# An S4D and SwiGLU block in which the rows' first inputs move into buffers whose contents are dead

## The chip, the cores and the metric

The kernel runs on one core of one Trainium2 chip, in one launch. The metric is the device time of that launch in microseconds (us). Before the change three runs gave a median of 976.74 us (975.26 to 977.07). Engines are TensorE (PE, with PEld for its weight loads), VectorE (DVE), ScalarE (ACT), GpSimd (POOL) and SyncE (SP), which here only issues DMAs. Each works through its own queue in order; between engines they wait on semaphores.

## The reference

One adaLN block over 2048 tokens of 640 channels, with 128 complex states for each channel and 1728 hidden units, all in fp32:

```python
mod = (silu(c) @ w_mod).reshape(1, 6, 1, -1)
sa, ca, ga, sb, cb, gb = mod rows
h = layernorm(x) * (1 + ca) + sa
K[d, l] = 2 Re sum_n C[d, n] dt[d] exp(A[d, n] dt[d] l)
y = irfft(rfft(h, 2L) * rfft(K, 2L))[:L] + h * D_skip
x = x + ga * y
h = layernorm(x) * (1 + cb) + sb
x = x + gb * ((silu(h @ w1) * (h @ w3)) @ w2)
```

The convolution runs along the tokens, the normalisations and the gated product along the channels. All of the first half (all channels' convolutions) for a token is needed before its second normalisation.

## The kernel before, in words

*Convolution.* The 640 channels are done in five blocks of 128 (b4 is the last, number 4). For each block the kernel's taps are made in eight chunks on POOL, ACT and DVE from exponential tables E (lines 517 and 565; one pair of tables for blocks of even number, one for odd), TensorE sums them over the states (kps), and the taps and the normalised input xb go through a first transform (ps), a spectrum (fh, fk), a product on DVE (hz, fp) and the first half of the inverse (fz). Its result zt is stored to HBM as zd, eight tiles for a block. xb, the spectral buffer sp, and the modulation rows rw lie in a pool named core.

*Rows.* The second half of the inverse works by tokens. zd is loaded again, token-wise. In the first part four inputs, iz0 to iz3 (u = 0 to 3, two row tiles each, so iy0 to iy7), serve token blocks 0 and 1 of 512 tokens each; TensorE multiplies them by wd (iy), DVE adds the result to the tokens x2 (ia), and statistics for the second normalisation are taken (BN, the is tasks). iy covers the channels of the first four channel blocks (cut = 512); the fifth block's 128 channels come last, by the reload izb0 and izb1, two loads of four DMAs each that wait for the last stores of zd, then iyb and iab. Then come the reciprocal root (rs), xn, the transposes tp, the modulation v, and the split of x into a high and a low part (x0h and x0l and so on), since each fp32 product is made of three: high by high, low by high, high by low.

*The feed-forward part.* Up tiles of 128 hidden units (numbers 0 to 12, and 13 with 64) are loaded raw (wr), split into wh and wl, and multiplied (gu); then th, a and ah are the gate, and acc the down product with w2, split likewise. The first two tiles (0 and 13) run plain for blocks 0 and 1 before all weights go through combined sums in larger groups.

*What sets the order.* Up to the start of those groups a list scheduler, Plan (line 167), decides: each task has an engine, a duration, predecessors, a rank (smaller goes first among those that are ready at nearly the same time) and rings of buffers that it takes and gives. Tasks of tail_tasks (line 1044) carry their ranks in the code. A tile framework then puts in the waits that data, buffers and reused memory require, so memory that is opened where another pool was closed waits for that pool's last reader. DMA issues use eight semaphores: a DMA on SP can wait for the landing of the eighth before it. Loads made by load (line 1060) are paced besides (line 1035): load n waits for the landing of load n-2 while n is under 6, then of load n-4, up to LOADS. Three steps structure the end of the plan: `change` closes the pools of the table work and opens xp, wp and ip for the rows; `border` closes ip, inv and core and opens the pools of the feed-forward part; in between run the last spectra.

Before the change, x2[0] and wd0 are loaded while block 4's chunks are made, everything else of the rows after `change`: iz0, iz1, up tile 0, up tile 13, x2[1], wd1, iz2 in this order, all paced (iz0 and iz1 are eight DMAs, an up tile two). iz3 goes after `border` into x3h and x3l, tiles of x that are not yet in use, so that iy6 and iy7 (u = 3) run after the transposes of block 0:

```python
early = j < 6
([] if early else ["tp0.4"]), rank if early else 16.7
```

x2 of block 1 is prepared by prepare(1, 31), that is with a rank behind the gates of block 0.

Of the kernel before, what the change touches and what calls it, by code (L numbers as in the profile page):

```python
# [10 lines left out]
F32 = mybir.dt.float32  # L11
F32R = mybir.dt.float32r
I32 = mybir.dt.int32
# [17 lines left out]
LOADS = 21  # L31
# [249 lines left out]
class K:  # L281
# [65 lines left out]
    def ln_end(self, pool, st, mv, tag):  # L347
# [169 lines left out]
    def table_sets(self):  # L517

        G = self.nc.gpsimd
        self.tabs, self.E = [], []  # L520
        self.j8 = self.tbl.tile([P, 8], F32, name="j8")
        for j in range(8):
            G.memset(self.j8[:, j:j + 1], float(j))
        for i in range(2):
            p1, p2 = (self.tbl.tile([P, HB2, 2, n], I32, name=f"p{n}{i}") for n in (8, 4))
            G.memset(p1[:, :, :, 0], 0)
            self.tabs.append((p1, p2))
            self.E.append((self.tbl.tile([P, P, 2, 8], F32, name=f"e1{i}"), self.tbl.tile([P, P, 3, 4], F32, name=f"e2{i}")))
        self.step = self.tbl.tile([P, 3, 2, HB2], I32, name="step")
# [514 lines left out]
    def tail_tasks(self, border, cut):  # L1044
# [15 lines left out]
        def load(name, src, dst, size, after=(), **kw):  # L1060
            i = n_load[0]
            n_load[0] += 1
            loads.append(name)
            early = i < LOADS
            add(name, "SP", 0, lambda: self.paced(dst(), src), ["change", *after] + (loads[max(i - 2, 0):i][:1] if early else ["izb0"]), -60 + .1 * i,
                dma=[size * (.62 if early else 1.0)], **kw)
        loads = []

        def load_x2(b):
            for q in range(4):  # L1070
                s = slice(q * 32, q * 32 + 32)
                load(f"lx{b}.{q}", self.xv[q, :, 4 * b:4 * b + 4, :], lambda b=b, s=s: self.x2[b][s], 327680)

        def load_wd(i):
            load(f"lwd{i}", self.t_wd[:, 4 * i:4 * i + 4], lambda: self.wd[i], 262144)
# [38 lines left out]
        for q in range(4):  # L1114
            s = slice(q * 32, q * 32 + 32)
            add(f"lx0.{q}", "SP", 0, lambda q=q, s=s: self.nc.sync.dma_start(self.x2[0][s], self.xv[q, :, :4, :]), [f"g{b4}.{q}.ph"], -400, dma=[327680])
        add("lwd0", "SP", 0, lambda: self.nc.sync.dma_start(self.wd[0], self.t_wd[:, :4]), [f"g{b4}.4.ph"], -400, dma=[262144])
        load_z(0)
        load_z(1)
        load_up(0)  # L1120
        load_up(13)
        load_x2(1)
        load_wd(1)
        load_z(2)

        def raw_split(m, rank, after=None):
            names = [f"lu{m}.{i}" for i in range(2)]
# [26 lines left out]
        def rows(b, rank):  # L1154
            for j in range(4 * b, 4 * b + 4):
                u = j // 2
                early = j < 6

                def inv(j=j, u=u, early=early):
                    py = bank[j] = self.pbank(f"iy{j}") if early else self.acc_bank(f"iy{j}", j % 4)  # L1160
# [4 lines left out]
                def plus(j=j):  # L1165
# [3 lines left out]
                    ([f"{x}{b4}.{i}.e" for x in ("hh", "k") for i in range(8)] if b == 0 else []) + (["z4.3.z"] if j in (4, 5) else []) + ([] if early else ["tp0.4"]), rank if early else 16.7, take=[("bank", 1)] if early else [])  # L1169
                add(f"ia{j}", "DVE", .69, plus, [f"iy{j}"], rank, give=[("bank", f"iy{j}")] if early else [])  # L1170
# [5 lines left out]
        add("border", None, 0, border, ends + [f"ia{j}" for j in range(6)] + ["change"], 0)  # L1176
# [23 lines left out]

        def ln_rest(b):
            ln[b] = self.ln_end(self.fp, *self.stats[b], f"n{b}")
# [9 lines left out]
        def prepare(b, rank):  # L1212
# [3 lines left out]
            add(f"ln{b}", "DVE", 3.9, lambda: ln_rest(b), [f"isb{b}"] + [f"is{j}.{c}" for j in range(4 * b, 4 * b + 4) for c in range(2)], rank)  # L1216
            for j in range(4):
                add(f"xn{b}.{j}", ("ACT", "DVE"), (.91, .62), lambda e, j=j: xn.__setitem__((b, j), self.norm(b, j, *ln[b], e)), [f"ln{b}"], rank + .01 * j)
            for k in range(KT):
                r = rank + .1 + .1 * k  # L1220
# [14 lines left out]
                add(f"tp{b}.{k}", "PE", .88, tp, [f"xn{b}.{j}" for j in range(4)] + [f"tp{b}.{k - 1}"] * (k > 0) + ([f"ia{4 + j}" for j in range(4)] + ["iab1"] if b else []), r)  # L1235
# [4 lines left out]
        prepare(1, 31)  # L1240

        def plain(b, tiles, p, rank, after):
# [23 lines left out]
            for r, m in enumerate(tiles):  # L1266
                gates(b, m, banks, f"{b}.{m}", last, names, (rank if b else 30) + .5 + .1 * r)
# [245 lines left out]
    def run(self):  # L1513
# [3 lines left out]
        self.wk, self.wz = c.tile([P, 2, P], F32, name="wk"), c.tile([P, 2, P], F32, name="wz")  # L1517
        self.dsk = c.tile([P, NB, E4], F32, name="dsk")
# [14 lines left out]
        core = self.core = open_("core", "right")  # L1533
        self.wb = core.tile([P, 32, P], F32, name="wb")
# [4 lines left out]
        self.wd = [x0.tile([P, 4, 2, 64], F32, name="wd0")]  # L1539
        self.x2 = [x0.tile([P, 4, D], F32, name="x20")]  # L1540
# [602 lines left out]
```

## Time and profile before

| What | Before |
|---|---|
| median of the runs | 976.74 us |
| lowest and highest of three | 975.26, 977.07 us |
| the profiled execution | 979.65 us |
| its span | 977.9 us |
| its mean granted TensorE clock | 0.969 |
| bytes moved | 127.31 MB |

The profiled execution is one run of its own; every duration that is quoted comes from it. In the rows a busy time is followed by "x" and the number of instructions, a timeline gives start, length and the group that ran, and the square bracket behind it gives the idle time of the engine just before, with what ended it. An operation is written out<-in by the program's names. The TensorE clock is the share of full speed that was granted.

### The profile page before, as it was taken

Reading aid. Unit: us, or ns where it says so; the run is one execution under the profiler, and the core shown is the slowest. Engines: PE = TensorE matmul, PEld = TensorE weight load, DVE = VectorE, ACT = ScalarE, POOL = GpSimd, SP = SyncE. Lnnn points to the kernel's source line nnn. Section 1 sums busy time; section 2 is a strip of 40 time slices with the busy share of each in tenths; the row PEclk is TensorE's granted clock in tenths of the full one; section 3 lists DMA queues with packets and bytes.
Section 4 is the critical chain, followed back from the end, with each engine's and each line's share of the span. In section 5 each row is a group of like instructions: output and inputs, shape, how many; then the busy total and the mean of one; then the engine's idle time right before and its main releaser. Section 6 shows DMA issues by size and latency. Waiting matters only on the chain.

```text
span 977.9 us, 20556 instructions
## 1 busy us (share of the span) xinstructions
PE 864.3 (88%) x7985; PEld 683.7 (70%) x7985; DVE 699.2 (72%) x1393; ACT 547.5 (56%) x1024; POOL 342.6 (35%) x371
## 2 busy tenths in 40 slices
PE   1463787779899997889999999999999999999997
PEld 1132665767788883667777778878778888888776
DVE  7998899999999957886767767557456464645322
ACT  6877788979888841564444445346434443443312
POOL 1797789879899600002112111000012112120000
PEclk9986898999999997899999999999999999999999
DMA  9955453623235269847345421265442323220374
GB/s 216 276 170 195 107 130 92 174 67 89 51 86 126 69 167 250 202 121 238 112 122 161 122 93 62 89 188 189 135 112 77 99 69 102 80 83 28 108 217 133
DMA packets 110506, 127.31 MB, mean 130 GB/s; under 512 B 10568, under 2 KB 90696, under 8 KB 109128
## 3 DMA queue, kind: packets, MB, share of 16 engines
q1 hardware_dynamic: 109032, 125.21, 45.3%
q8 instruction: 63, 1.03, 0.5%
q10 hardware_dynamic: 1376, 0.79, 0.3%
q14 instruction: 35, 0.29, 0.1%
HBM read 95.82 MB, written 30.15 MB: 129 GB/s over the span
## 4 chain that ended last, share of the span: by engine, by line
PE 70%; DVE 15%; ACT 6%; DMA 4%; issue 3%; POOL 1%; SPq 1%; DVEq 0%; ACTq 0%
PE c L156 19%; PE acc L156 18%; PE X L156 12%; PE ps L156 4%; PE gu L156 3%; DVE yy L156 3%; PE kps L156 3%; PE fk L156 3%; PE fz L156 2%; PE fh L156 2%; DVE hn L156 2%; DVE fp L156 2%; DVE xx L156 2%; ACT tr L156 2%; PE iy L156 1%
## 5 line engine op out<-in xcount | busy, mean ns | idle before, releaser
L156 PE MATMUL acc<-ah,w 128*128 128x512 f32 x560 | 173.2, 395 | 2.7 <-DMA w<-w2d 1.9
L156 PEld LDWEIGHTS acc<-ah,w 128*128 128x128 f32 x560 | 103.7, 188 | 26.1 <-issue 2.3
L156 PE MATMUL acc<-al,w 128*128 128x512 f32 x260 | 101.9, 392 | 0.0
L156 POOL TENSOR_TENSOR yy<-e,e 128x512 f32<-128x512 f32 x80 | 86.3, 1095 | 18.8 <-PE kps L156 15.2
L636 DVE TENSOR_TENSOR wl<-s,wh 128x256 fp32r<-128x256 f32 x92 | 38.9, 423 | 68.2 <-ACT wh L635 67.8
L812 POOL TENSOR_TENSOR s<-wr 128x256 f32<-128x256 f32 x22 | 16.7, 760 | 188.5 <-DVE wl L636 91.3
L635 ACT ACTIVATE wh<-s 128x256 fp32r<-128x256 f32 x92 | 37.6, 410 | 79.2 <-PE X L156 58.5
L156 POOL TENSOR_TENSOR ph<-p,p 128x1024 int32<-128x1024 int32 x40 | 78.9, 1972 | 6.7 <-ACT tr L156 6.4
L156 PE MATMUL kps<-yy,xx 128*32 128x64 f32 x2560 | 51.4, 234 | 29.0 <-DVE xx L156 21.4
L156 DVE TENSOR_TENSOR yy<-yy,tr 128x512 f32<-128x512 f32 (+1 forms) x80 | 75.4, 945 | 0.9 <-ACT tr L156 0.6
L156 PEld LDWEIGHTS kps<-yy,xx 128*32 128x32 f32 x2560 | 45.0, 117 | 38.9 <-issue 22.8
L635 ACT ACTIVATE wh<-wr 128x256 fp32r<-128x256 f32 x92 | 38.3, 418 | 56.5 <-PE X L156 43.2
L813 POOL TENSOR_TENSOR s<-s,wr 128x256 f32<-128x256 f32 x22 | 16.6, 754 | 133.2 <-issue 133.2
L873 ACT ACTIVATE t<-g 128x512 f32<-128x512 f32 x44 | 27.8, 632 | 52.7 <-DVE g L837 52.7
L156 ACT ACTIVATE tr<-ph,hpi 128x512 f32<-128x512 f32 x80 | 54.7, 691 | 3.9 <-DVE xx L156 2.2
L156 PEld LDWEIGHTS acc<-al,w 128*128 128x128 f32 x260 | 48.8, 188 | 11.0 <-DVE al L636 0.3
L842 DVE SCALAR_TENSOR_TENSOR g<-t,g 128x512 f32<-128x512 f32 x48 | 33.7, 702 | 31.3 <-ACT t L873 29.3
L156 DVE TENSOR_TENSOR xx<-tr,xx 128x512 f32<-128x512 f32 x80 | 54.5, 682 | 1.0 <-ACT tr L156 1.0
L156 ACT ACTIVATE tr<-ph 128x512 f32<-128x512 int32 x80 | 47.3, 598 | 13.2 <-DVE yy L156 7.4
L156 PE MATMUL ps<-wk,xb 128*64 128x128 f32 x640 | 48.1, 305 | 6.0 <-ACT sp L156 3.3
L156 PE MATMUL ps<-wk,ks 128*64 128x128 f32 x640 | 41.9, 283 | 12.9 <-DVE ks L156 8.1
L156 PEld LDWEIGHTS ps<-wk,xb 128*64 128x64 f32 x640 | 44.6, 221 | 10.8 <-ACT sp L156 4.6
(435 smaller groups left out, 2347.0 us busy)
## 6 DMA issues: line engine op xcount, KB each, us to landing
w<-w2d SPq DMA_DIRECT2D x42, 640.0 KB, 4.0
wr<-in_w SPq DMA_DIRECT2D x52, 320.0 KB, 3.9
zd<-zt SPq DMA_DIRECT2D x40, 256.0 KB, 3.0
w2d<-w SPq DMA_DIRECT2D x14, 640.0 KB, 3.6
xs<-in_x SPq DMA_DIRECT2D x16, 320.0 KB, 11.5
hs<-hb SPq DMA_DIRECT2D x20, 256.0 KB, 2.5
xb<-hs SPq DMA_DIRECT2D x20, 256.0 KB, 4.5
x<-in_x SPq DMA_DIRECT2D x16, 320.0 KB, 10.1
```

The costliest lines, as they stand in the source:

```text
L156: self.prev = self.k.order(f(*a, **kw), self.prev)
L635: self.nc.scalar.activation(H, v, AF.Copy)
L636: eng.tensor_tensor(Lo, v, H.bitcast(F32), op=ALU.subtract)
L812: eng.tensor_tensor(s[0], u[:, 0:2], u[:, 2:4], op=ALU.add)
L813: eng.tensor_tensor(s[1], s[0], g[:, 0:2], op=ALU.subtract)
L842: V.scalar_tensor_tensor(g, th, 1.0, g, op0=ALU.add, op1=ALU.mult)
L873: tanh = lambda o, i: A.activation(o, i, AF.Tanh, scale=0.5)
```

## The change

Three regions that are dead by then take data of the rows, and some tasks are put in another place:

- The tables of odd blocks, last used for block 3, now lie in a tile named late (3584 values for each partition) in pool x0. Behind block 3's last chunk this tile takes x2[1] (the first 2560) and wd0 and wd1. x2[0] is loaded while block 3's chunks are made, x2[1], wd0 and wd1 while block 4's are. wd2 and wd3 are issued right behind them.
- Up tile 0 is loaded raw into rw once the input of block 4 has been normalised, ahead of all iz, and its split no longer shares the ring wr.
- iz3 goes into xb, after the spectra of block 4 have been issued, so that iy6 and iy7 run with the other iy, before the reload; `border` waits for all eight ia and for the five splits of tile 0.
- wk, wz and dsk move from the pool const to core. LOADS is 20 in place of 21.
- The root of the normalisation is cut into steps (one task for block 0, four for block 1); prepare(1) gets rank 16.85, its transposes tp1 go by that rank and the rest of it one later; the gates of block 0's tiles 0 and 13 get rank 17 (G0); the sums T1 wait for these gates.

By the instruction order of the two builds, the engines' order stays as it was up to the last transforms of block 4, apart from the added loads on SP. There the five splits of tile 0 (ACT, DVE) stand among the last ps. tp1.0 stands after the fourth of the five steps of block 0's product, and tp1.1 to tp1.4 right after it; the 15 acc of the first down tile come behind block 1's product; on ACT the two high parts of w2 stand before xn of block 0, and the wh of tile 13 before the fifth hz of block 4.

```diff
-LOADS = 21
+LOADS = 20
+G0 = 17
...
+    def ln_mean(self, st, mv):
         for j in range(4):
             self.nc.vector.bn_aggr(mv[:, j, :], st[:, j, :, :])
+
+    def ln_end(self, pool, st, mv, tag):
+        self.ln_mean(st, mv)
         return self.rsqrt(pool, mv[:, :, 1], 4, tag, (mv[:, :, 0], -1.0))
+
+    def ln_steps(self, pool, mv, tag):
+
+        V = self.nc.vector
+        v, w, t = (pool.tile([P, 4], F32, name=f"rs_{x}_{tag}", tag=f"rs_{x}") for x in "vwt")
+        y, nb = (pool.tile([P, 4], F32, name=f"rs_{x}_{tag}", tag=f"rs_{x}", bufs=2) for x in "yn")
+        wi = w.bitcast(I32)
+
+        def first():
+            V.tensor_scalar(v, mv[:, :, 1], 1.0, EPS, op0=ALU.mult, op1=ALU.add)
+            V.tensor_scalar(wi, v.bitcast(I32), 1, None, op0=ALU.logical_shift_right)
+            V.tensor_scalar(wi, wi, -1.0, float(0x5F3759DF), op0=ALU.mult, op1=ALU.add)
+
+        def newton(i):
+            V.tensor_mul(t, w, w)
+            V.scalar_tensor_tensor(t, t, -0.5, v, op0=ALU.mult, op1=ALU.mult)
+            V.scalar_tensor_tensor(y if i == 2 else w, t, 1.5, w, op0=ALU.add, op1=ALU.mult)
+            if i == 2:
+                V.scalar_tensor_tensor(nb, mv[:, :, 0], -1.0, y, op0=ALU.mult, op1=ALU.mult)
+        return (y, nb), [first] + [lambda i=i: newton(i) for i in range(3)]
...
+            if i:
+                e = self.spare
+                self.E.append((e[:, :2048].rearrange("p (d m j) -> p d m j", m=2, j=8), e[:, 2048:].rearrange("p (d m j) -> p d m j", m=3, j=4)))
+            else:
+                self.E.append((self.tbl.tile([P, P, 2, 8], F32, name="e10"), self.tbl.tile([P, P, 3, 4], F32, name="e20")))
...
-                z[u] = [t.bitcast(F32) for t in self.x_new(f"x{u}", f"iz{u}", 2)]
+                z[u] = [self.xb[:, 1024 * pr:1024 * pr + 1024].rearrange("p (a d) -> p a d", a=2) for pr in range(2)]
-                    load(f"iz{u}.{pr}{h}", zv[:, t0:t0 + 2, :cut], dst, 262144, done + (["border"] if u > 2 else []))
+                    load(f"iz{u}.{pr}{h}", zv[:, t0:t0 + 2, :cut], dst, 262144, done + ([f"hh{b4}.{i}.m" for i in range(8)] if u > 2 else []))
...
+                    if m == 0:
+                        raw[m] = self.rw.rearrange("p a (k f) -> p a k f", k=KT)
...
-                     [f"wl{0 if m == 1 else 13}.{i}" for i in range(5 if m == 1 else 3)] if m in (1, 2) else [])
+                     [f"wl13.{i}" for i in range(3)] if m == 2 else [f"h{b4}.{i}.a" for i in range(4)] if m == 0 else [], "inv" if m == 0 else "change")
...
+        used = [f"g{b4 - 1}.7.z{i}" for i in range(3)] + [f"mag{b4 - 1}", f"exp{b4 - 1}"]
+        for b, src in ((0, b4 - 1), (1, b4)):
+            old = used if b else []
+            for q in range(4):
+                s = slice(q * 32, q * 32 + 32)
+                add(f"lx{b}.{q}", "SP", 0, lambda b=b, q=q, s=s: self.nc.sync.dma_start(self.x2[b][s], self.xv[q, :, 4 * b:4 * b + 4, :]),
+                    [f"g{src}.{q}.ph"] + old, -400, dma=[327680])
+            if b == 0:
+                continue
+            for i in range(2):
+                add(f"lwd{i}", "SP", 0, lambda i=i: self.nc.sync.dma_start(self.wd[i], self.t_wd[:, 4 * i:4 * i + 4]), [f"g{src}.4.ph"] + old, -400, dma=[262144])
+        load_up(0)
         load_z(0)
         load_z(1)
-        load_up(0)
         load_up(13)
-        load_x2(1)
-        load_wd(1)
         load_z(2)
+        load_z(3)
...
-                early = j < 6
-
-                def inv(j=j, u=u, early=early):
-                    py = bank[j] = self.pbank(f"iy{j}") if early else self.acc_bank(f"iy{j}", j % 4)
+
+                def inv(j=j, u=u):
+                    py = bank[j] = self.pbank(f"iy{j}")
...
-        add("border", None, 0, border, ends + [f"ia{j}" for j in range(6)] + ["change"], 0)
+        add("border", None, 0, border, ends + [f"ia{j}" for j in range(8)] + ["change"] + [f"wl0.{i}" for i in range(5)], 0)
...
-        load_z(3)
         load_down(0)
...
+            add(f"lm{b}", "DVE", .8, mean, [f"isb{b}"] + [f"is{j}.{c}" for j in range(4 * b, 4 * b + 4) for c in range(2)], rank)
+            if b == 0:
+                add("ln0", "DVE", 3.1, lambda: [f() for f in steps[0]], ["lm0"], rank)
+            for i in range(4 if b else 0):
+                add(f"ln{b}" if i == 3 else f"ln{b}.{i}", "DVE", .8 if i == 3 else .6, lambda i=i: steps[0][i](), [f"ln{b}.{i - 1}" if i else f"lm{b}"], rank + .01)
...
-                r = rank + .1 + .1 * k
+                r = rank + .1 + .1 * k + b
...
-        prepare(1, 31)
+        prepare(1, 16.85)
...
-                gates(b, m, banks, f"{b}.{m}", last, names, (rank if b else 30) + .5 + .1 * r)
+                gates(b, m, banks, f"{b}.{m}", last, names, (rank if b or m == 1 else G0) + .5 + .1 * r)
...
-            sums("T1", i, (1, 0), (0, 0), 41 + i, ["ia4", "ia5"])
-            sums("T2", i, (1, 2), "T1", 43 + i, ["ia6", "ia7"])
+            sums("T1", i, (1, 0), (0, 0), 41 + i, ["gl0.0", "gl0.13"])
+            sums("T2", i, (1, 2), "T1", 43 + i, [])
...
+        self.wk, self.wz = core.tile([P, 2, P], F32, name="wk"), core.tile([P, 2, P], F32, name="wz")
+        self.dsk = core.tile([P, NB, E4], F32, name="dsk")
...
-        self.wd = [x0.tile([P, 4, 2, 64], F32, name="wd0")]
-        self.x2 = [x0.tile([P, 4, D], F32, name="x20")]
+        self.spare = x0.tile([P, 3584], F32, name="late")
+        self.wd = [self.spare[:, 2560 + 512 * i:3072 + 512 * i].rearrange("p (a b c) -> p a b c", a=4, b=2) for i in range(2)]
+        self.x2 = [x0.tile([P, 4, D], F32, name="x20"), self.spare[:, :2560].rearrange("p (j d) -> p j d", j=4)]
...
-            self.wd += [self.xp.tile([P, 4, 2, 64], F32, name=f"wd{i}", tag="ha", bufs=4) for i in range(1, 4)]
-            self.x2.append(self.xp.tile([P, 4, D], F32, name="x21"))
+            self.wd += [self.xp.tile([P, 4, 2, 64], F32, name=f"wd{i}", tag="ha", bufs=4) for i in range(2, 4)]
```

More of the change, by code (lines that the diff above doesn't have):

```diff
@@ L1058, in tail_tasks, with load @@
         n_load = [0]
-        def load(name, src, dst, size, after=(), **kw):
+        def load(name, src, dst, size, after=(), pool="change", **kw):
             i = n_load[0]
@@ L1064, in load @@
             early = i < LOADS
-            add(name, "SP", 0, lambda: self.paced(dst(), src), ["change", *after] + (loads[max(i - 2, 0):i][:1] if early else ["izb0"]), -60 + .1 * i,
+            add(name, "SP", 0, lambda: self.paced(dst(), src), [pool, *after] + (loads[max(i - 2, 0):i][:1] if early else ["izb0"]), -60 + .1 * i,
                 dma=[size * (.62 if early else 1.0)], **kw)
         loads = []
[L1069 to L1075, printed above, removed]
         def z_tiles(u):
@@ L1112, in load_down @@
                      [f"w2l{0 if m == 1 else 13}"] if m in (1, 2) else [])
[L1114 to L1117, printed above, removed]
+        used = [f"g{b4 - 1}.7.z{i}" for i in range(3)] + [f"mag{b4 - 1}", f"exp{b4 - 1}"]
[10 more added lines that the diff above has]
+        load_up(0)
         load_z(0)
         load_z(1)
-        load_up(0)
         load_up(13)
-        load_x2(1)
-        load_wd(1)
         load_z(2)
+        load_z(3)
         def raw_split(m, rank, after=None):
-            names = [f"lu{m}.{i}" for i in range(2)]
+            names = [f"lu{m}.{i}" for i in range(2)] + ["change"]
             n = 3 if m == 13 else 5
@@ L1168, in rows @@
                 add(f"iy{j}", "PE", .54, inv, [f"iz{u}.{x}" for x in ("00", "01", "10", "11")] + [f"lwd{b}", *[f"lx{b}.{q}" for q in range(4)]] +
-                    ([f"{x}{b4}.{i}.e" for x in ("hh", "k") for i in range(8)] if b == 0 else []) + (["z4.3.z"] if j in (4, 5) else []) + ([] if early else ["tp0.4"]), rank if early else 16.7, take=[("bank", 1)] if early else [])
-                add(f"ia{j}", "DVE", .69, plus, [f"iy{j}"], rank, give=[("bank", f"iy{j}")] if early else [])
+                    ([f"{x}{b4}.{i}.e" for x in ("hh", "k") for i in range(8)] if b == 0 else []) + (["z4.3.z"] if j > 3 else []), rank, take=[("bank", 1)])
+                add(f"ia{j}", "DVE", .69, plus, [f"iy{j}"], rank, give=[("bank", f"iy{j}")])
                 for c in range(2):
@@ L1215, in prepare, with mean @@
             add(f"isb{b}", "DVE", 1.15, lambda: last_stats(b), [f"iab{b}"], rank)
-            add(f"ln{b}", "DVE", 3.9, lambda: ln_rest(b), [f"isb{b}"] + [f"is{j}.{c}" for j in range(4 * b, 4 * b + 4) for c in range(2)], rank)
+            steps = {}
+            def mean():
+                self.ln_mean(*self.stats[b])
+                ln[b], steps[0] = self.ln_steps(self.fp, self.stats[b][1], f"n{b}")
+            add(f"lm{b}", "DVE", .8, mean, [f"isb{b}"] + [f"is{j}.{c}" for j in range(4 * b, 4 * b + 4) for c in range(2)], rank)
[3 more added lines that the diff above has]
+                add(f"ln{b}" if i == 3 else f"ln{b}.{i}", "DVE", .8 if i == 3 else .6, lambda i=i: steps[0][i](), [f"ln{b}.{i - 1}" if i else f"lm{b}"], rank + .01)
             for j in range(4):
```

8 lines of the change are left out of this document (1 added, 7 removed).

## The prediction

> **What bounds the kernel now.** I read the page's totals first, then windows over the stretch that the change touches, then the chain of waits there, and last the timelines of single engines.
>
> ```profile
> span 977.9 us, 20556 instructions
> PE 864.3 (88%) x7985; PEld 683.7 (70%) x7985; DVE 699.2 (72%) x1393; ACT 547.5 (56%) x1024; POOL 342.6 (35%) x371
> ```
>
> TensorE is the busiest engine, so the next question is where it is not busy. In the windows the columns are the stretch, its length, then busy time of PE, PEld, DVE, ACT and POOL, the granted clock, the DMA share and GB/s.
>
> ```profile
> 200.00:300.00 100.00, 90.61 (x1948) 76.73 (x1950) 96.66 (x175) 86.10 (x147) 91.27 (x89) 1.00 0.33 84
> 360.00:370.00 10.00, 10.00 (x138) 7.71 (x134) 9.39 (x20) 5.43 (x13) 0.00 (x0) 1.00 0.98 257
> 370.00:380.00 10.00, 7.43 (x29) 2.61 (x28) 7.58 (x21) 1.19 (x2) 0.00 (x0) 1.00 1.05 256
> 380.00:390.00 10.00, 6.51 (x26) 2.87 (x28) 5.58 (x22) 0.00 (x0) 0.00 (x0) 0.57 0.83 225
> 390.00:400.00 10.00, 5.66 (x35) 5.09 (x32) 8.24 (x31) 4.75 (x7) 0.63 (x1) 0.67 1.12 270
> 410.00:420.00 10.00, 8.82 (x47) 6.83 (x45) 6.45 (x10) 8.86 (x13) 0.00 (x0) 1.00 0.59 170
> 420.00:430.00 10.00, 8.46 (x30) 6.83 (x31) 9.04 (x17) 7.42 (x15) 0.00 (x0) 0.83 0.37 93
> 430.00:500.00 70.00, 70.00 (x308) 53.69 (x307) 50.13 (x104) 30.38 (x63) 12.75 (x15) 1.00 0.49 154
> 500.00:600.00 100.00, 100.00 (x439) 75.78 (x438) 71.37 (x172) 45.67 (x95) 17.12 (x23) 1.00 0.38 113
> 700.00:800.00 100.00, 98.33 (x436) 79.88 (x435) 58.29 (x108) 44.01 (x96) 19.23 (x26) 1.00 0.31 88
> ```
>
> From 430 on TensorE has no gap for 170 us, and later the largest gap in 100 us is the 1.7 of 700:800, whose work and loads would move along: whatever brings the first work of this stretch forward brings the end forward by as much. Before it, between 370 and 430, lie the hand-over from the convolution to the rows and half-rate stretches. Up to 343 us compute engines keep order and waits; only loads are added there. The chain of waits (start, length, what) names the hand-over:
>
> ```profile
> 373.77 4.87 DMA zd<-zt
> 378.69 0.05 issue
> 378.73 0.05 DVEq L156
> 378.83 0.70 DVE zt L156
> 379.54 3.15 DMA zd<-zt
> 382.76 3.38 DMA izb<-zd
> ...
> 395.24 0.91 ACT xn L156
> ...
> 400.99 2.28 PE iy L156 x8
> 403.27 10.54 PE gu L156 x45
> ```
>
> The store of 373.77 frees its buffer in the ring of three zt when it lands, at 378.64; the copy that waits for that buffer follows, its store leaves at 379.54, and only when that has landed does the reload izb start, at 382.76. The reload lands, iyb and iab0 follow, then statistics, xn, transposes, the iy of the fourth input, and the first product gu.
>
> **The change part by part.**
>
> *Early loads.* x2[0], x2[1], two wd and the first up tile (some 4 MB, of which x2[0] and one wd went out early before too) go out between about 225 and 304 us, in SP's queue ahead of fetches xb<-hs and of stores. That stretch has DMA share 0.33, DVE 96.66 of 100. Lower bound 0. Upper bound: one x load of 320 KB at the 257 GB/s of 360:370 is 1.3 us in front of a fetch. I take 0, since the share leaves two thirds free, and keep 0 to +1.3.
>
> *Pieces of the first up tile.* The eight wl_u of before run in the last product's stretch:
>
> ```profile
> 345.41 1.32 PE L156 MATMUL kps<-yy,xx 128*32 128x64 f32 x64
> 343.73 11.53 SPq L156 DMA_DIRECT2D iz<-zd  x8
> iz<-zd SPq DMA_DIRECT2D x12, 256.0 KB, 4.5
> 352.32 0.69 DVE L156 TENSOR_TENSOR fp<-fk,hz 128x512 f32<-128x512 f32 x1 [4.97 <-PE fk L156]
> 360.81 0.60 ACT L156 ACTIVATE hz<-fh 128x512 f32<-128x512 f32 x1 [1.44 <-PE fh L156]
> L156 DVE TENSOR_TENSOR wl_u<-wr,wh_u 128x256 fp32r<-128x256 f32 (+1 forms) x8 | 3.1, 399 | 0.0
> 396.75 0.86 DVE L156 BATCH_NORM_STATS2 st<-x 128x6 f32<-128x128 f32 x4
> ```
>
> Five of these eight go into DVE's 4.97 us idle before 352.32, where they cost nothing: 5 x 0.40 = 2.0 us leave a DVE that is busy 9.39 of 10. Coming in ahead of the last product are ia0 and two BN: 0.68 + 2 x 0.21 = 1.1. Against that, two waits are new. First, iz0's buffer now lies over the last table chunk's tiles: iz0 can start only after kps ends, 345.41 + 1.32 = 346.73, and not at 343.73 (+3.0). Second, ACT has wh of tile 13 queued ahead of the fifth hz (360.81). Loads are paced, each waiting for the fourth one before: iz0 346.75, its second half one landing (4.5) later, 351.3, iz1 right behind, tile 13 another landing later, about 357.3, landed about 361.8; its wh (0.41) ends about 362.2, so hz is 1.4 late, and behind it the products fk, fp and fz. Bounds: 0 (landing before 360.8) to +3.
>
> *The last product and the reload.* 2.0 freed, 1.1 and 1.4 put in: fp of z4.2 ends about where it did. But now both last fz follow each other with no iy between (one iy pair is 1.08 us), the zt of z4.2 I put at 372.7, 1.0 earlier than 373.77. The ring's wait then costs a landing: 4.87 before; x2 is no longer in flight, but iz3 is, four loads that SP issues straight ahead of these stores. Page median of the stores is 3.0; I take 4.2. Copy 0.7 more gives a last store at about 377.7, landing in about 3.0: reload at 380.8, 2.0 earlier than 382.76. Bounds: 0 (landings as before, hz late) to -4 (landings of 3.0, hz in time).
>
> *Between reload and xn.* Reload to iab0 stays 390.38 - 382.76 = 7.6:
>
> ```profile
> 390.38 0.69 DVE L156 TENSOR_TENSOR x<-iyb,x 128x512 f32<-128x512 f32 x1 [0.73 <-PE iyb L156]
> 388.40 3.47 PE L156 MATMUL iyb<-izb,wd 128*64 128x128 f32 x30 [1.03 <-DMA izb<-zd]
> 396.20 4.79 PE L156 MATMUL tp<-ident,xn 128*128 128x128 f32 x20 [4.33 <-ACT xn L156]
> ```
>
> DVE now has all eight ia and some 22 BN to do first: from 378.3, 7 x 0.64 + 22 x 0.2 = 8.9, until 387.2; iab0 by the reload is 388.4, so this just hides; it would cost if the reload were over 1.2 faster. Six more BN of block 1 stand between iab0 and the root, at 0.21: +1.2. ACT also has two w2 highs before xn, whose loads are issued right behind the reload; that took 395.24 as xn's start, and they need about 9.4 us from the reload's issue (three issues at 0.6 and a 4.77 landing behind its landing) where xn needs 13.7: hidden by 4 us. xn: -2.0 + 1.2 = -0.8.
>
> *The fourth input.* xb lands before the reload, so iy6 and iy7 no longer stand between transposes and gu: -2.28. Their cover is TensorE's idle (7.43 and 6.51 of 10 busy). gu0 starts -0.8 - 2.28 = -3.1, near 400.1.
>
> *Clock.* At which rate gu0 begins:
>
> ```profile
> 391.50:395.00 3.50, 0.37 (x4) 0.12 (x1) 3.08 (x19) 0.00 (x0) 0.00 (x0) 0.99 1.03 241
> 396.20:401.00 4.80, 4.79 (x22) 4.13 (x24) 3.90 (x10) 4.66 (x8) 0.00 (x0) 0.50 1.16 286
> 401.00:403.30 2.30, 2.30 (x9) 0.60 (x9) 1.63 (x3) 2.17 (x4) 0.00 (x0) 0.83 1.01 211
> ```
>
> After the pause the 20 tp run at 0.50, and the rate returns within the iy: 0.83 as the mean of 2.3 us is 0.8 us at half, so at 401.8, 5.6 us after 396.20. Without the iy, gu0 starts 4.8 after tp, so 0.8 us of it run at half rate: +0.4. Bounds: 0 (after iyb's start at 388.40 the rate was back by 391.50, 3.1 us later) to +1.9 (both delays one after the other, 8.7 us, of which gu0 meets 3.9). The Trainium skill, "TensorE: Matmul & The Clock Gate", Part 1: The HAM clock gate, says that the array falls to half rate after an idle window of about 3.4 us and recovers after a busy one, with a free-running window; the trace's 4.33 us pause and 5.6 us return agree, and by that rule a return takes at most two windows, so gu0 would lose at most half of 6.8 - 4.8, +1.0 (an estimate).
>
> *Block 1.* Its xn no longer waits for iy6/iy7, tp1.0 comes inside gu0, and gates of tile 13 are ranked differently.
>
> ```profile
> 416.42 0.50 PE L156 MATMUL gu<-x4h,wh_u 128*128 128x512 f32 x1 [0.45 <-ACT x4h L156]
> 417.15 0.50 PE L156 MATMUL gu<-x4l,wh_u 128*128 128x512 f32 x1 [0.22 <-DVE x4l L156]
> 421.54 0.51 PE L156 MATMUL gu<-x4l,wh_u 128*128 128x512 f32 x1 [2.05 <-DVE x4l L156]
> 422.40 0.63 PE L156 MATMUL gu<-x4l,wh_u 128*128 128x512 f32 x1
> ```
>
> Stalls of 0.45 + 0.22 + 2.05 = 2.7, then about 3 us at half rate (0.63 for a matmul, and 0.83 as the window's mean), worth 1.5: 4.2 in all. What remains: ACT still has table load, th0.0, th0.13 and a before the second x4h; from gu0's end that is about 3.1 us, TensorE is covered for 2.0 (16 tp) + 2.1 (a quarter of the product). I take 1.3 of the 4.2 as left: -2.9; bounds -4.2 to -0.7. The 15 acc of the first down tile move behind the product: no change, as they run either way.
>
> *Sum against the profiled execution* (979.65 us, span 977.9): early 0, reload -2.0, BN +1.2, iy -2.3, clock +0.4, block 1 -2.9: -5.6. That is 974.05; the profiled execution stood 2.9 over the median of the runs, 976.74, so **971.1 us** for the runs.
>
> **Rivals.**
>
> *The reload comes no earlier* (hz late as tile 13 lands, or the ring's landing stays 4.87). For: DMA is 0.98 to 1.05 busy there, and iz3's four loads stand directly ahead of the stores. Against: some 1.4 MB less to move between 360 and the reload (x, wd and half of the up tile are out, 2.4 MB; iz3 is in, 1.0). Sum without -2.0: gain 3.6, 973.1.
>
> *DVE becomes the bound of block 1.* It is 8.24, 6.45 and 9.04 of 10 in 390, 410 and 420; the same work squeezed into 6 us less would leave about no idle. Then the block 1 term is -0.7, and the sum -3.4: 973.3. Against: some seven ia and BN leave this stretch for the one before.
>
> *Slower: ACT held by tile 13's load.* Place: wh of tile 13 ahead of the fifth hz. In before no hz waits for a load. The price is the lateness of that landing over 360.8, about 1:1 from 361 on, since TensorE and DVE are both full there and every fz hangs on hz.
>
> ```profile
> xs<-in_x SPq DMA_DIRECT2D x16, 320.0 KB, 11.5
> ```
>
> With an issue at 357.3 and the 11.5 us that loads of x took, landing is 368.8 and hz 369.2, 8.4 late against the 1.4 in the sum: 7.0 more, 971.1 + 7.0 = 978.1. It decides from a landing of about 10 us (break-even) or 12 (slower by 0.2%, were the other terms also at their worse ends, 10). For: 160 KB in pieces of 256 bytes. Against: iz took 4.5 in the same stretch, and x no longer shares the queue.
>
> *Nothing changes*: all terms but iy and BN fall out: -2.3 + 1.2 + 0.4 = -0.7, 976.0. For it: every hand-over from store to reload remains.
>
> **How the numbers follow.** The forecast gets 0.62, the late reload 0.14, DVE's bound 0.09, the held ACT 0.10, nothing 0.05. The range 967.5 to 976.0 takes in the better ends of reload (-2 more) and block 1 (-1.3 more), and at the top both first rivals and "nothing". Within 0.2% (about 1.95 us), what a measurement can tell from no change, lies 974.8 to 978.7: "nothing", and part of the held ACT. Faster 0.85, same 0.06, slower 0.09, that last being the held ACT with one more term at its worse end.
>
> **What would show it.** The last store should leave between 376 and 379 and the reload between 379 and 382; no iy between tp and gu0; gu0 near 400, gu1 without a 2 us stall, and its end near 426 in place of 431; from there on no gap. iz starts at 346.7. If the fifth hz ends later than 363, the tile 13 wait counts for more. Wrong would be a reload after 383, or an xn with w2r's landing as its real releaser, or gaps of TensorE between 430 and 600.

## The result, and the profile after

The changed kernel is slower. Its median is 983.09 us (981.28 to 983.82, four runs) against 976.5 us of the kernel before on the same chip (975.26 to 977.07): a ratio of 1.0067, 95% interval 1.0048 to 1.0085. The forecast was 971.1 us. The hand-over came out at the predicted sum, though not by the predicted parts; what makes the kernel slower lies behind it, in a stretch that the prediction had taken as moving along unchanged.

The first rows of the page, after:

```profile
span 979.5 us, 20551 instructions
PE 870.5 (89%) x7985; PEld 683.7 (70%) x7985; DVE 700.9 (72%) x1395; ACT 546.8 (56%) x1022; POOL 341.9 (35%) x371
```

TensorE has the same 7,985 matmuls as before and takes 6.2 us more for them (870.5 against 864.3). Windows of the kernel after, with the columns of the prediction:

```profile
370.00:380.00 10.00, 8.83 (x40) 3.19 (x40) 7.90 (x22) 1.19 (x2) 0.00 (x0) 1.00 0.62 165
380.00:390.00 10.00, 5.17 (x40) 3.16 (x36) 8.47 (x35) 0.74 (x1) 0.63 (x1) 0.80 0.93 201
390.00:400.00 10.00, 6.50 (x26) 5.71 (x26) 9.32 (x36) 7.33 (x11) 0.00 (x0) 0.51 1.10 251
410.00:420.00 10.00, 8.04 (x40) 5.78 (x39) 7.43 (x13) 9.86 (x18) 0.00 (x0) 1.00 0.70 225
420.00:430.00 10.00, 10.00 (x45) 8.05 (x44) 9.87 (x19) 7.11 (x15) 0.00 (x0) 1.00 0.00 0
500.00:600.00 100.00, 100.00 (x433) 74.65 (x432) 69.52 (x169) 45.48 (x94) 16.73 (x22) 1.00 0.36 111
800.00:900.00 100.00, 100.00 (x430) 80.58 (x429) 56.16 (x108) 42.14 (x93) 15.67 (x21) 1.00 0.25 73
```

The last of these windows, before:

```profile
800.00:900.00 100.00, 100.00 (x437) 81.87 (x436) 57.38 (x110) 43.31 (x97) 15.55 (x21) 1.00 0.24 73
```

Between 410 and 430 the kernel after is better: the half-rate stretch is gone (0.83 before, 1.00 now). But from 500 to 600 it does 433 matmuls where 439 ran, and from 800 to 900 430 where 437 ran. TensorE is fully busy in both, at a granted clock of 1.00 in both, with hardly changed DMA traffic. A matmul simply takes longer: 100 / 437 = 0.2288 us against 100 / 430 = 0.2326. I call the time from the start of one matmul to the start of the next its period. Taken over all periods of neighbouring 128x512 matmuls between 440 and 960 us in the two traces (some 2,050 each, those between 200 and 260 ns), the mean is 229.4 ns before and 233.3 after. The busy share cannot show this; the count in a full window does.

The chain of waits, after (start, length, what):

```profile
376.42 3.25 DMA zd<-zt
...
380.55 4.80 DMA izb<-zd
...
392.64 0.93 ACT xn L157
...
398.41 9.04 PE gu L157 x36
...
415.63 9.57 PE gu L157 x39
425.20 3.50 PE acc L157 x15
```

The last store leaves at 376.42, gu begins near 398, the first acc at 425.2; before, these were 379.54, 403.27 and 431.43. Single engines, after, ACT first:

```profile
361.67 0.42 ACT L157 ACTIVATE wh_u<-wr 128x256 fp32r<-128x256 f32 x1 [2.91 <-DMA wr<-in_w]
362.00 0.58 ACT L157 ACTIVATE hz<-fh 128x512 f32<-128x512 f32 x1
392.64 1.73 ACT L157 ACTIVATE xn<-x,rs_n_n,rs_y_n 128x640 f32<-128x640 f32 x2 [1.20 <-DVE rs_n_n L157]
```

and TensorE:

```profile
393.62 4.80 PE L157 MATMUL tp<-ident,xn 128*128 128x128 f32 x20 [3.50 <-ACT xn L157]
407.29 0.60 PE L157 MATMUL tp<-ident,xn 128*128 128x128 f32 x4
412.06 0.50 PE L157 MATMUL gu<-x4h,wh_u 128*128 128x512 f32 x1 [0.33 <-DVE a L157]
413.37 0.50 PE L157 MATMUL gu<-x4h,wh_u 128*128 128x512 f32 x1 [0.35 <-DVE a L157]
415.63 0.47 PE L157 MATMUL gu<-x4h,wh_u 128*128 128x512 f32 x1 [1.29 <-DVE a L157]
```

The fifth hz does wait for up tile 13's load (it starts at 362.00 instead of 360.81), and block 1's product still stalls, 0.33 + 0.35 + 1.29 = 2.0 us.

To set apart what comes before the hand-over, I count from the end of the last kps (346.73 before, 346.12 after). The first acc comes 84.5 us later before and 78.9 after: -5.6. From the first acc to the end of TensorE's work it is 541.3 before and 549.2 after: +7.9. With the earlier end of kps, -0.6, that gives the +1.6 by which the two spans differ (977.9 and 979.5; the parts are rounded). The whole loss of the profiled execution is in the tail.

### The profile page after: what moved, and what is told of

It is laid out like the page before. It is cut to its first block, busy times and chain, and to the rows that moved or that the text cites. A ratio compares the mean times of both kernels' runs of the same rounds, so it can differ in the third digit from the quotient of the medians.

```text
span 979.5 us, 20551 instructions
## 1 busy us (share of the span) xinstructions
PE 870.5 (89%) x7985; PEld 683.7 (70%) x7985; DVE 700.9 (72%) x1395; ACT 546.8 (56%) x1022; POOL 341.9 (35%) x371
## 4 chain that ended last, share of the span: by engine, by line
PE 70%; DVE 16%; issue 4%; ACT 3%; DMA 3%; POOL 2%; SPq 1%; DVEq 0%; ACTq 0%; POOLq 0%
PE c L157 19%; PE acc L157 17%; PE X L157 12%; PE ps L157 4%; PE gu L157 3%; PE fz L157 3%; DVE yy L157 3%; PE kps L157 3%; PE fk L157 2%; PE fh L157 2%; DVE fp L157 2%; DVE hn L157 2%; DVE xx L157 2%; DVE xb L157 1%; PE iy L157 1%
## 5 line engine op out<-in xcount | busy, mean ns | idle before, releaser
L157 PE MATMUL acc<-ah,w 128*128 128x512 f32 x560 | 175.2, 398 | 2.2 <-DMA w<-w2d 1.6
L157 PEld LDWEIGHTS acc<-ah,w 128*128 128x128 f32 x560 | 103.8, 188 | 27.6 <-issue 2.0
L157 DVE TENSOR_TENSOR yy<-yy,tr 128x512 f32<-128x512 f32 (+1 forms) x80 | 75.5, 946 | 1.2 <-ACT tr L157 0.6
L841 POOL TENSOR_TENSOR s<-s,wr 128x256 f32<-128x256 f32 x22 | 16.8, 762 | 136.2 <-issue 136.2
L157 POOL TENSOR_TENSOR yy<-e,e 128x512 f32<-128x512 f32 x48 | 52.4, 1108 | 9.7 <-PE kps L157 3.7
```

The costliest lines, as they stand in the source:

```text
L157: self.prev = self.k.order(f(*a, **kw), self.prev)
L841: eng.tensor_tensor(s[1], s[0], g[:, 0:2], op=ALU.subtract)
```

## The experiments

**What the build does to addresses.** The tiles of wk, wz and dsk leave const (1,024 + 1,024 + 640 = 2,688 bytes for each partition), late replaces wd0 in x0 (14,336 - 2,048), and x2[1] leaves xp (10,240). So pool wp, where all weight tiles lie, begins 2,688 - 12,288 + 10,240 = 640 bytes lower. The streamed tiles (x, ah, al) lie in the pool ffn; their starts modulo 256 stay. Modulo 256 a shift by 640 is one by 128. Below, "distance" is the start of the streamed tile less that of the weights, modulo 256, from the addresses that the build assigns: 64 before, 192 after.

Theory A: this distance sets the matmul's period. Theory B: the slower matmuls come from the new instruction order, from traffic beside them or from the clock. One unused tile between xp and wp tells them apart, since it moves nothing but wp (and ip, which holds iz):

```diff
-            self.xp, self.wp, self.ip = open_("xp"), open_("wp"), open_("ip")
+            self.xp = open_("xp")
+            open_("shift").tile([P, 32], F32, name="shift")
+            self.wp, self.ip = open_("wp"), open_("ip")
...
-        close("ps", "po", "ffn", "wp", "xp", "x0")
+        close("ps", "po", "ffn", "wp", "shift", "xp", "x0")
```

Width 32 is 128 bytes; 64, 96, 16, 48 and 40 are used below. The order on all five engines is the same with and without the tile.

**e1: the changed kernel, 128 bytes.**

> The changed kernel with one unused tile of 128 bytes for each partition between the pools xp and wp: every weight tile (and iz) lies 128 bytes higher, nothing else moves. Weights then start at the same place modulo 512 as before the change. Theory A (the place of the weight tiles against the streamed tiles sets the period of a matmul): from 440 us on the mean start-to-start time of the 128x512 matmuls falls from 233.3 to about 229.4 ns, some 1,950 of them, so -7.6 us: 975.5 us, and below before if the hand-over's 6 us hold (970 to 976). Theory B (the slower matmuls come from the other instruction order, from DVE, ACT or DMA traffic beside them, or from the clock): period stays 233, time 981 to 984.

**e2: the kernel before, 128 bytes.**

> The kernel before with the same 128 bytes between xp and wp; instruction order and transfers are those of before. Theory A: the weights then stand 448 bytes modulo 512 from the streamed tiles (192 modulo 256, as in the changed kernel), the period rises from 229.4 to about 233.3 ns and the time by about 7.6 us, to 984. Theory B: unchanged, 976.5.

**e3 and e4: the changed kernel, 256 and 384 bytes.**

> The changed kernel with 256 bytes between xp and wp. If only the place modulo 256 counts, it is as slow as the changed kernel (period 233.3); if modulo 512, it is a third place, period open between 226 and 236. Theory B: 233.3.

> The changed kernel with 384 bytes between xp and wp. If the place modulo 256 counts, it is as fast as with 128 bytes (229.4); if modulo 512, a fourth place, open. Theory B: 233.3.

One window of each says it. e1, e2, e3 and e4, in this order:

```profile
800.00:900.00 100.00, 100.00 (x438) 82.06 (x437) 54.68 (x104) 40.83 (x89) 14.82 (x20) 1.00 0.25 74
```

```profile
800.00:900.00 100.00, 100.00 (x431) 80.62 (x430) 54.70 (x105) 42.37 (x93) 17.19 (x23) 1.00 0.27 79
```

```profile
800.00:900.00 100.00, 100.00 (x430) 80.55 (x429) 54.97 (x105) 42.77 (x94) 17.19 (x23) 1.00 0.25 78
```

```profile
800.00:900.00 100.00, 100.00 (x438) 82.05 (x437) 57.32 (x109) 42.92 (x94) 14.75 (x20) 1.00 0.24 73
```

438, 431, 430, 438: fast, slow, slow, fast, as theory A has it. e1 is faster than the kernel before, 973.76 against 978.15 us, ratio 0.9954 (0.9942 to 0.9967); e2, the kernel before with nothing but 128 unused bytes, is slower, 986.27, ratio 1.0091 (1.0064 to 1.0118). e3 took 985.07 and e4 976.85 us, in one execution each. Theory B falls: the order was that of the changed kernel in e1 and that of before in e2. 256 bytes leave the period as it was, and 384 do what 128 do: with these placements what counts repeats after 256 bytes.

**e5, e9, e10: other distances.** e5 is the changed kernel with 64 bytes; e9 and e10 have 192 and 160 bytes on top of e8 (below).

> The changed kernel with 64 bytes between xp and wp: the streamed tiles then stand 128 modulo 256 from the weights (64 with 128 bytes: 229.1 ns; 192 without: 233.3). Theory A leaves the value open between 226 and 236 ns; it says only that the place decides, so first acc to the end of TensorE's work takes 540 to 549 us, in step with the period (about 2.0 us for each ns).

> As e8 (up tile 13 loaded first), with 192 bytes between xp and wp in place of 128: streamed tiles and weights then start at the same place modulo 256. Measured so far, by their distance modulo 256: 64 gives 229.1 ns, 128 gives 232.4, 192 gives 233.3. Open between 226 and 236; if a shorter distance is better, below 229. The time from the first acc to the end of TensorE's work follows with about 2.1 us for each ns.

> As e8, with 160 bytes between xp and wp: distance 32 modulo 256, weights at a multiple of 64. If only the distance counts, between the values at 0 and at 64; if a weight address that is no multiple of 64 was what the fast cases share, slower than both.

The same window of e5, e9 and e10:

```profile
800.00:900.00 100.00, 100.00 (x432) 81.09 (x431) 56.39 (x108) 42.73 (x95) 15.50 (x21) 1.00 0.24 73
```

```profile
800.00:900.00 100.00, 100.00 (x443) 82.81 (x442) 52.64 (x101) 40.28 (x89) 14.72 (x20) 1.00 0.24 73
```

```profile
800.00:900.00 100.00, 100.00 (x430) 80.32 (x429) 56.15 (x108) 41.91 (x93) 15.50 (x21) 1.00 0.24 73
```

| Distance modulo 256 | Kernels | Mean period, ns | First acc to end of PE, us |
|---|---|---|---|
| 0 | e9, e12 | 227.3, 227.3 | 536.4, 536.5 |
| 32 | e10 | 233.3 | 549.0 |
| 64 | before, e1, e4, e6, e7, e8, e11 | 229.1 to 229.4 | 540.0 to 541.3 |
| 128 | e5 | 232.4 | 546.7 |
| 192 | after, e2, e3 | 233.3, 233.2, 233.3 | 549.2, 548.8, 548.9 |

(Periods and times are worked out from the traces as above; e5, e9 and e10 took 980.62, 969.03 and 980.93 us, in one execution each.) The kernel before holds one case more within itself: the streamed tiles of x3hT and x3lT start at another place there (distance 96), against the same weights. 128 of its matmuls stream them, at 233.2 ns; the other 1,942 take 229.1. So it is not the place of the weights alone, and not the traffic beside the matmuls, which both kinds share. e7 below, where these tiles again lie as before, repeats it: 233.1 against 229.1 ns. In e2, where the weights lie 128 bytes higher, the same 128 matmuls have distance 224 and take 232.5 ns. Why 0 and 64 are fast and 32, 96, 128, 192 and 224 slow isn't settled. The period at 32 doesn't lie between those at 0 and 64, as the expectation of e10 had it for the case that the distance alone counts. But e10 is also the only run with the weights at a multiple of 64 bytes, so it can't tell the one from the other. Distance 160 wasn't tried.

**e6: the ranks of block 1 put back, with 128 bytes.**

```diff
-G0 = 17
+G0 = 30
...
-        prepare(1, 16.85)
+        prepare(1, 31)
```

> The changed kernel with 128 bytes between xp and wp, and with block 1's preparation and the gates of tiles 0 and 13 at the ranks of before (31 and 30). By the prediction's block 1 term the first acc comes 2.9 us later after the end of the last kps (78 to 80 us with the changed ranks, so 81 to 83), with a stall of about 2 us in block 1's product; the start of gu does not move. If instead the block 1 gain comes from the inputs being there early, the ranks cost nothing when put back.

TensorE in e6:

```profile
408.86 2.35 PE L157 MATMUL tp<-ident,xn 128*128 128x128 f32 x20
411.50 0.51 PE L157 MATMUL gu<-x4h,wh_u 128*128 128x512 f32 x1 [0.30 <-ACT x4h L157]
412.40 0.50 PE L157 MATMUL gu<-x4l,wh_u 128*128 128x512 f32 x1 [0.39 <-DVE x4l L157]
416.62 0.50 PE L157 MATMUL gu<-x4l,wh_u 128*128 128x512 f32 x1 [1.88 <-DVE x4l L157]
```

The stall is there as expected, 0.30 + 0.39 + 1.88 = 2.6 us, but the first acc comes 77.3 us after kps, no later than in e1 (77.7), and not at the expected 81 to 83; gu to first acc takes 26.3 us, where the kernels with the new ranks and the early input take 25.9 to 27.6. Its one execution took 971.85 us. The ranks exchange one stall for another and bring nothing that these runs show.

**e7: the fourth input late, with 128 bytes.** iz3 goes into x3h and x3l after `border`, and iy6 and iy7 behind the transposes, as before the change:

```diff
-                z[u] = [self.xb[:, 1024 * pr:1024 * pr + 1024].rearrange("p (a d) -> p a d", a=2) for pr in range(2)]
+                z[u] = [t.bitcast(F32) for t in self.x_new(f"x{u}", f"iz{u}", 2)]
...
-        load_z(3)
         load_down(0)
         load_down(13)
...
+                early = j < 6
...
+ ([] if early else ["tp0.4"]), rank if early else 16.7
```

The removed load_z(3) stands ahead of the two down loads again, and LOADS is 16.

> The changed kernel with 128 bytes between xp and wp, and with the fourth input loaded after border into x3h and x3l as before, so that iy6 and iy7 stand behind the transposes (16 paced loads in place of 20). Prediction's term: tp to gu takes 7.0 in place of 4.4 us (2.3 to 2.6 later). The loads of iz3 no longer stand ahead of the last stores: if they delay these, the reload comes earlier by up to 1 us against the end of kps; if not, it stays at 33 to 34 us after it. First acc 2 to 3 us later than with iz3 early.

tp to gu takes 6.6 us (4.4 in e1), and gu to first acc 28.0 (26.6 in e1); the stalls of before are back:

```profile
417.76 0.50 PE L157 MATMUL gu<-x4h,wh_u 128*128 128x512 f32 x1 [0.44 <-ACT x4h L157]
418.48 0.50 PE L157 MATMUL gu<-x4l,wh_u 128*128 128x512 f32 x1 [0.22 <-DVE x4l L157]
422.88 0.52 PE L157 MATMUL gu<-x4l,wh_u 128*128 128x512 f32 x1 [2.06 <-DVE x4l L157]
```

First acc is at 82.3 us, 4.6 later than in e1. Of this, 1.8 us lie ahead of iab0, where e9 and e12, one and the same kernel, differ by 1.6. From iab0 to the first acc e7 takes 40.5 us, e1 37.7, and all kernels with the early input 36.4 to 38.6. Against e1 these 2.8 are the 2.2 of iy and 1.4 between gu and the first acc, less 0.85 for the six BN that the early input puts ahead of xn: as expected, 2 to 3. The 28.0 from gu to first acc are those of before (28.1) although the ranks are the new ones, so what I had put down to the ranks comes from the early input. The reload is at 33.9 us after kps (33.1 in e1), not earlier, so iz3's loads do not hold up the last stores. (Its one execution took 980.46 us; besides the 4.6, its last kps ended 2.4 us later than e1's.)

**e8: up tile 13 loaded first, with 128 bytes.**

```diff
         load_up(0)
+        load_up(13)
         load_z(0)
         load_z(1)
-        load_up(13)
```

> The changed kernel with 128 bytes between xp and wp, and with up tile 13 loaded ahead of iz0 and iz1, so that its wh on ACT waits for no load when the fifth hz is due. The prediction has that wait at 1.4 us: fifth hz should end 14.7 us after the end of kps as before the change (16 to 17 with the change), and the reload come up to 1.4 earlier. If DVE or the ring of zt sets the last store, the reload does not move. Time against the kernel before: -4.4 with 128 bytes alone, so -4.4 to -5.8 here.

ACT in e8:

```profile
359.89 0.60 ACT L157 ACTIVATE hz<-fh 128x512 f32<-128x512 f32 x1 [1.44 <-PE fh L157]
```

Now fh releases the fifth hz, as before the change: it ends 14.8 us after kps (16.0 in e1). The reload comes at 32.7 (33.1 in e1), first acc at 78.9 (77.7): 0.4 us gained and more than that lost again behind it. That is within the scatter: e9 and e12 have their first acc at 79.1 and 75.5. 971.71 us, ratio 0.9943 (0.9926 to 0.9961) against 0.9954: no gain that the runs can tell.

**e11: the early loads issued later, with 128 bytes.** The planned tasks stay, so the order on PE, DVE, ACT and POOL does too; only the issues move: those of x2[0] to the tasks of x2[1], those of up tile 0 behind wd.

```diff
-lambda b=b, q=q, s=s: self.nc.sync.dma_start(self.x2[b][s], self.xv[q, :, 4 * b:4 * b + 4, :])
+lambda b=b, q=q, s=s: [self.nc.sync.dma_start(self.x2[i][s], self.xv[q, :, 4 * i:4 * i + 4, :]) for i in range(2 * b)]
```

> The changed kernel with 128 bytes between xp and wp; the loads of x2[0] and of up tile 0 are issued with those of x2[1] and wd at about 285 to 300 us, not at 222 to 248 us. The order on PE, DVE, ACT and POOL is unchanged. The prediction took the early loads as free (0 to 1.3 us). If they cost time by holding up PE (kps is cut in two near 255 us, with a wait that nothing in the trace releases), that cut is gone and the stretch around it is about 1.0 us shorter, as before the change; 1.0 us less in all, unless the heavier traffic at 285 to 300 us costs as much. If they are free, nothing changes: about -4.4 us against before.

TensorE near 255 us in e1, and then before:

```profile
253.90 0.87 PE L157 MATMUL kps<-yy,xx 128*32 128x64 f32 x43 [1.07 <-DVE xx L157]
255.45 0.64 PE L157 MATMUL kps<-yy,xx 128*32 128x64 f32 x21 [0.67 <-issue]
```

```profile
253.62 1.15 PE L156 MATMUL kps<-yy,xx 128*32 128x64 f32 x64 [1.05 <-DVE xx L156]
```

A window of e1 around it:

```profile
250.00:256.00 6.00, 4.26 (x114) 3.83 (x110) 6.00 (x9) 4.78 (x8) 1.95 (x1) 1.00 0.82 191
```

With the early loads the 64 kps are cut in two; TensorE stands still although nothing in the view holds it. From the start of these kps to the start of the next 64, 6.9 to 7.0 us pass before, in e2 and in e11, and 7.5 to 8.3 in most kernels with the early loads: +0.5 to +1.3. In the changed kernel itself (9.8) and in e10 (9.4) the granted clock falls to half right behind the cut, and the loss is 2.9 and 2.5. The changed kernel:

```profile
253.00:256.00 3.00, 3.00 (x32) 3.00 (x32) 1.52 (x4) 3.00 (x6) 3.00 (x4) 0.50 0.03 5
```

In e11 the cut comes back where its loads now are, and worse:

```profile
305.00:310.00 5.00, 4.75 (x109) 4.29 (x98) 3.88 (x9) 3.63 (x6) 4.21 (x4) 1.00 1.01 230
310.00:315.00 5.00, 2.40 (x68) 2.23 (x69) 4.28 (x9) 0.38 (x1) 3.65 (x5) 0.68 0.57 176
```

```profile
312.60 1.95 PE L157 MATMUL kps<-yy,xx 128*32 128x64 f32 x62 [2.84 <-issue]
```

2.84 us of standing still behind a window with a DMA share of 1.01, and then the granted clock drops: seven xx steps on, this stretch is 5.9 us longer than in the others. In all, 974.48 us, ratio 0.9937 (0.9917 to 0.9958), which can't be told from e1. The last kps of its profiled execution ends at 351.4 us, later than in any other run, but the timed runs don't show that either place of the loads is the better one. Neither is free.

What TensorE waits for can be read from the DMA packets of the traces. One queue carries instructions alone, in packets of 16,384 bytes:

```profile
q8 instruction: 63, 1.03, 0.5%
```

TensorE's instructions in the trace are 16,144, so 63 packets come to 256 of them each. In the 14 traces TensorE has 25 waits of over 0.4 us that the profile puts down to nothing ("issue"), and all are at one of three places, with 6,337, 8,385 or 8,641 of its instructions ahead of them. These are 2,048 and 256 apart, whole numbers of packets. (The one at 8,385 is in every kernel, also before: 1.22 us ahead of 305.42.) In each of the 25 it goes on 1.3 to 1.7 us after a packet of this queue has ended. In e11 that packet runs from 310.00 to 311.09, 8.3 us behind the one before it, in the middle of the standing still from 309.76 to 312.60. So TensorE had run out of instructions. That their packet was late because of the loads rests on its moving with them.

**e12: e9 timed.** Up tile 13 first and 192 bytes, everything else as in the changed kernel.

> The kernel of e9 again, timed in rounds: up tile 13 loaded ahead of iz0 and iz1, 192 bytes between xp and wp. By the parts measured so far against the kernel before: hand-over to the first acc -6 us, early loads +0.5 to +1, matmul period 227.3 in place of 229.4 ns about -4.5 us; in all about -9 to -10 us, a ratio near 0.990. If only the single look was lucky: near the -5.6 of e8.

967.86 us against 977.11, ratio 0.991 (0.9891 to 0.9928): faster than the kernel before, and by the ratios (0.991 and 1.0067) than the changed one. Its page begins:

```profile
span 965.3 us, 20549 instructions
PE 853.7 (88%) x7985; PEld 679.5 (70%) x7985; DVE 701.0 (73%) x1395; ACT 545.8 (57%) x1022; POOL 340.1 (35%) x371
```

The same 7,985 matmuls take 16.8 us less than in the changed kernel (870.5): 12.9 of it from the first acc on, by the place of the weight tiles. The other 4 lie ahead of it, where the granted clock differs between executions, and aren't taken apart further.

## Why the prediction was wrong

Point by point, after against before, counted from the end of the last kps:

| Step | Predicted | Measured |
|---|---|---|
| fifth hz late by up tile 13's load | 1.4 | 1.8 (e1 to e4: 1.3 to 2.1) |
| reload | -2.0 | -2.4 |
| reload to iab0 | 0 | -0.4 |
| iab0 to xn (six BN) | +1.2 | +0.9 |
| tp to gu (iy out) | -2.3 | -2.6 |
| gu to first acc: clock +0.4, block 1 -2.9 | -2.5 | -1.1 |
| first acc | -5.6 | -5.6 |
| early loads | 0, at most +1.3 | +2.9 around 255 us (+0.5 to +1.3 in most of the others) |
| first acc to the end | 0 | +7.9 |

**The step that failed** is the sentence ahead of the sum: after 430 us TensorE "has no gap", so "whatever brings the first work of this stretch forward brings the end forward by as much". That holds only if each matmul takes as long as before. I read the windows for gaps and never asked whether the operands of some 2,000 matmuls still lay where they had lain, though the diff moves three tiles out of one pool and 12 KB into another ahead of the weights. It isn't a term mis-sized, it is a term that is missing: +3.9 ns x some 2,000 matmuls = +7.8 us. e1 and e2 show it from both sides.

**Luck in the sum.** The -5.6 is met to a tenth because the parts' errors cancel: block 1 and the clock brought 1.4 us less, and the other four parts 1.4 more. It is also one execution: in the five with this order of instructions (after, e1, e3, e4, e5) the first acc comes 77.7 to 80.0 us after kps, against 84.5 and 85.0 with the order of before (before, e2). A gain of 4.5 to 7.3 is shown, not one of 5.6.

**Right for the reasons given:** the zt of z4.2 (372.8, predicted 372.7), the fourth input's 2.3 us, the six BN, hidden w2 highs (xn waits for DVE's rs, not for w2r), no gap from 430 to 600.

**Right in direction, wrong in size:** the last store left at 376.4 and not at 377.7, since the store that frees the ring's buffer landed after 2.3 us (372.81 to 375.15) where I took 4.2; the ring's wait, 2.1 us of DVE before, is gone altogether. Block 1 brought less. I had 1.3 of 4.2 us left; 2.0 are left as stalls, and gu's start ran at half rate for longer than the 0.8 us that I took (0.72 as the mean of 398 to 401 us). And by e6 and e7 what it brought came from the early input, not from the ranks. The early loads cost more than their bound in the changed kernel's trace, and by another way than the one I priced: not a fetch of data behind them on SP's queue but TensorE's own instructions.

**The rivals.** Slower was right, but not by the mechanism that I gave it: up tile 13's load did hold ACT, by 2 us and not by 8, and e8 shows that even this costs next to nothing at the end. The other rivals were answers to a question that the result did not turn on.

**What stays open:** the measured medians differ by 6.6 us and the profiled executions by 1.6. Of these 5.0, 3.2 are that the profiled execution before was slower than its median and 1.8 that the one after was faster. In the profiled executions the tail, the hand-over and the early loads give 7.9 - 5.6 + 2.9 = 5.2, and the rest of the stretch up to the last kps -3.5. That stretch varies by several us from run to run (the last kps ends at 345.1 to 351.4 in these traces), with the granted clock among the reasons, and no run here separates a part of the change in the rest of it.

## What to carry to other kernels

When tiles move between pools, work out where the operands of the busiest matmuls now start, weights and streamed tiles both, and compare a count of matmuls in a fully busy window before and after: a share of 100% hides a period that has changed. Before believing or discarding a change that alters a kernel's memory map, run it with the weights' old place restored by an unused tile; here 128 bytes turned +0.67% into -0.46%, and 192 bytes with a reordered load into -0.9%. And loads put into a stretch where their data could wait are not free just because no engine waits for them: TensorE stood still behind a full DMA window without any semaphore to show for it, for want of instructions. Such a wait shows by its place, at a multiple of 256 instructions from the others, and by the packets of the instruction queue.

## What the runs showed of the hardware

The mean period of a 128x512 fp32r matmul with a new weight load each time was between 227.3 and 233.3 ns, by the starts of its two operands modulo 256 bytes, at a granted clock of 1.00 in the windows shown. The Trainium skill, "TensorE: Matmul & The Clock Gate", Part 2: What happens when you issue a matmul, has two independent SBUF read ports, so that loading the next weights takes no read bandwidth from the running matmul. The measured 2.6% between places show that the period does depend on where the two operands lie to each other; whether these ports have a part in it no run here shows.

TensorE waited 0.67 us (e1) and 2.84 us (e11) with nothing that releases it, in or right behind stretches with a DMA share of 0.82 to 1.01, each time a whole number of 256 instructions from the other such waits, and until 1.3 to 1.7 us after a packet of the instruction queue had ended. The Trainium skill, "Runtime: NRT & Kernel Launch", Instruction fetch mechanics, says that each sequencer fetches its instructions through a DMA queue of its own while it runs. The traces agree, by the 63 packets of 16,384 bytes and the 25 waits that lie whole packets apart; that the other transfers made the packets late rests on this, that moving the loads moved the wait (from 255 us in e1 to 310 us in e11).
